# One transformer block on one core: P times V as two row halves among the other half's scores, and 64x32 column tiles for scores, maxima and side products

## The chip, the cores and the metric

The kernel runs on one core of a Trainium2 chip. A time is the device time of one execution in microseconds (us). Before the change two executions took 1753.78 us each. One more execution was profiled; the lines marked as profile come from it. Engines are named as in the profile: PE (TensorE, matmuls), PEld (its weight loads), DVE (VectorE), ACT (ScalarE), POOL (GpSimd) and SP (the queue that starts most DMAs).

## The reference

One block with adaptive layer norm: 2048 tokens of width 512, attention of 32 heads of width 16 that all share one key head and one value head, and a bilinear feed-forward layer of width 1792. Everything is float32.

```python
mod = (silu(c) @ w_mod)                    # six rows: sa, ca, ga, sb, cb, gb
h = layernorm(x) * (1 + ca) + sa
q = (h @ wq) as 32 heads of 16;  k = h @ wk;  v = h @ wv     # one k, one v
p = softmax(q k^T / 4);  x = x + ga * (concat(p v) @ wo)
h = layernorm(x) * (1 + cb) + sb
x = x + gb * (((h @ w_gate) * (h @ w_up)) @ w_down)
```

## The kernel before, in words

The 2048 queries are four blocks of 512. A *unit* is four heads of one block, so there are 32 units, eight for each block. Inside a unit the loop runs over 16 key tiles of 128 keys.

Three kinds of work belong to each unit. First, the **maxima**: for each query row the largest score over all keys, found one unit ahead of its use (`max_mm`, L535). Products of 128 queries by 512 keys go into a bank `mx`, and DVE reduces each bank to one column (L544). Second, the **scores**, transposed, 128 keys by 512 queries for each head (`qk_exp`, L574): a product into a bank `sc` (L579), then ACT's exponential into the tile `P` in SBUF (L581). The maximum is subtracted inside the product, since two of the 50 contracted rows hold it. Third, **P times V** (`pv`, L583): for each key tile, four float32 products, one for each head, each with 32 columns of weights (16 of V, the others of ones for the row sums), accumulate in one bank `pv` (L588). At the end of the unit ACT copies that bank out (`pv_out`, L591), and DMAs carry the parts on.

Queries and keys are held twice in SBUF, on partitions 0 to 63 and 64 to 127, as high and low float16 halves, 48 or 50 rows each. A product of scores or maxima uses the rows of one copy (`a` = 0 or 1) and all 128 columns, so that two of them, one for each half of the rows, can share the array.

The rest, called **side products** here, is dense work: the query projection, the output projection `wo`, and the feed-forward layer. They are float16 in three terms (high by high, low by high, high by low). `duo` (L471) takes two result groups at a time, splits each product's contraction of 128 into two row halves (`half`, L467), and lets one row half work on one group's bank while the other works on the second's; at mid-way the two swap. `plain` (L496) does a product with all 128 rows.

The order is written out by hand: the engines run what the Python code issues, in that order. The main loop at the file's end takes 32 steps in each unit, two for each key tile. In a step it issues a maximum for rows 0, a score for rows 1, a score for rows 0 and a maximum for rows 1. After every second step comes P times V of the key tile before; after the others `fill_gap` (L1039) issues some side products, as many as a credit allows that grows with the work left before a due step (`pace`, L1018). `BURST` caps how many go at once. 38 steps of maxima alone (`LEAD`) run ahead of the main loop, and what is left of the side work, with all of block 3's feed-forward layer, runs behind it.

PSUM has eight banks: two for scores and one `spare` (a third for scores, or the second bank of a `duo`), three for maxima, one `misc`, one for P times V.

Of the kernel before, what the change touches and what calls it, by code (L numbers as in the profile page):

```python
# [31 lines left out]
NMX = 3  # L32
# [7 lines left out]
BURST = 6  # L40
LEAST = 4
# [11 lines left out]
def adaln_mqa_glu_kernel(ctx: ExitStack, tc: tile.TileContext, x_in, wq_in, wk_in, wv_in, wo_in,  # L53
# [20 lines left out]

    def ps_mx():
        return psum.tile([128, 512], F32, name="mx", tag="mx", bufs=NMX)

# [23 lines left out]
    for i in range(6, 8):  # L101
        xts.append(work.tile([128, 2, D], F32, name="P", tag="P", bufs=4))
# [363 lines left out]

    def half(p, g, i, r, start, stop):  # L467
        left, right = g.op(i)
        nc.tensor.matmul(p, left[64 * r:64 * r + 64], right[64 * r:64 * r + 64], start=start, stop=stop)  # L469
# [65 lines left out]
    def max_mm(u, i, a):  # L535
        kc, r = divmod(i, 8)
        p, t = divmod(r, 4)
        s = sst[u % 3]
        if i == 0 and a == 0:
            mparts[u] = work.tile([128, 2, 2, 4, 4], F32, name="mpart")  # L540
        m = ps_mx()
        nc.tensor.matmul(m, s[64 * a:64 * a + 48, p, t * 128:(t + 1) * 128],  # L542
                         kst[64 * a:64 * a + 48, kc * 512:(kc + 1) * 512], start=True, stop=True)
        nc.vector.tensor_reduce(mparts[u][:, a, p, t, kc:kc + 1], m, axis=AX.X, op=OP.max)  # L544
# [29 lines left out]
    def qk_exp(u, kt, p, a):  # L574
        s = sst[u % 3]
        if (u, kt, p) not in ptl:
            ptl[u, kt, p] = work.tile([128, 2, D], F32, name="P", tag="P", bufs=4)
        t = ps_sc()
        nc.tensor.matmul(t, kst[64 * a:64 * a + 50, kt * 128:(kt + 1) * 128],  # L579
                         s[64 * a:64 * a + 50, p, :], start=True, stop=True)  # L580
        nc.scalar.activation(ptl[u, kt, p][:, a, :], t, AF.Exp)  # L581

    def pv(u, kt):  # L583
        if kt == 0:
            pvb[u] = psum.tile([128, 512], F32, name="pv", tag="pv", bufs=1)
        for j in range(4):
            p, a = divmod(j, 2)
            nc.tensor.matmul(pvb[u][32 * j:32 * j + 32, :], vst[:, kt, :], ptl[u, kt, p][:, a, :],  # L588
                             start=(kt == 0), stop=(kt == KT - 1))

    def pv_out(u):  # L591
        b, g = divmod(u, UB)
        ev = work.tile([128, BT], F32, name="ev", tag="ev", bufs=3)
        nc.scalar.activation(ev, pvb[u], AF.Copy, scale=evs)  # L594
# [55 lines left out]
    def wo_work(b):  # L650
# [13 lines left out]
        def fin(t):  # L664
            def f(p):
                if b < NB - 1:
                    x1 = work.tile([128, D], F32, name="x1", tag="x1", bufs=4)
                else:
                    x1 = work.tile([128, D], F32, name="x1p", tag="P", bufs=4)
# [322 lines left out]
    def max_half(a):  # L992
        u, i = divmod(mstep[0], NSTEP)
        if a == 1:
            mstep[0] += 1
# [43 lines left out]
    def fill_gap(step):  # L1039
# [17 lines left out]
        if cur["one"]:  # L1057
            burst(step, max(1, min(int(credit[0]), cur["left"], MOST_ONE)))
            return
        turn = cur["turn"]  # L1060
        parts = max(-(-turn // BURST), min(round(turn / max(credit[0], 1.0)), turn // LEAST), 1)
        n = -(-turn // parts)
        if not cur["second"]:
            n = max(n, -(-cur["turn"] // max((NU * NSTEP - 2 - step) // 2, 1)))
# [64 lines left out]

    for u in range(NU):  # L1130
# [3 lines left out]
        for i in range(NSTEP):  # L1134
# [4 lines left out]
            max_half(0)  # L1139
            qk_exp(u, kt, p, 1)  # L1140
            drain_mids()
            qk_exp(u, kt, p, 0)
            max_half(1)
            if p == 1:
                if kt == 0:
                    if u > 0:
                        pv(u - 1, KT - 1)
                        posts.append(lambda u=u: pv_out(u - 1))
                else:
                    pv(u, kt - 1)  # L1150
                late_max()
            elif fill or cur["gen"]:
                credit[0] = min(credit[0] + pace(step), 9.0)
                one = cur["one"] if cur["gen"] else fill[0][1] == "one"
                if credit[0] >= (MOST_ONE if one else 1.0):
                    fill_gap(step)
            side_step(step)
            if u > 0 and g % 2 == 0 and i in (4, 8, 14):
                if i == 4:
                    nrm = normalise((u - 1) // UB, ((u - 1) % UB) // 2)  # L1160
                nrm[(4, 8, 14).index(i)]()
# [21 lines left out]
    pv(u, KT - 1)  # L1183
# [58 lines left out]
```

## Time and profile before

| what | value |
|---|---|
| the two timed executions | 1753.78 us and 1753.78 us |
| the profiled execution: span from first to last instruction | 1754.7 us |
| instructions in it | 32145, of them 12655 matmuls and 12655 weight loads |
| from the first P times V matmul to the last | 95.9 to 1603.3 us |
| PE busy | 1695.0 us, 97% |
| DVE busy | 1412.2 us, 80% |
| ACT busy | 1220.7 us, 70% |
| POOL busy | 505.0 us, 29% |
| the PE clock granted, mean | 0.988 |

The span is 0.9 us longer than the timed executions, 0.05%, and the view says nothing of time outside it. PE's busy time is the union of the times in which a matmul is under way, with ends that are modelled; 97% says that PE is hardly ever empty, not that it is at its peak. The timeline merges equal instructions that follow one another into one row: its start, its length, the engine, the line, the operation, the tiles, and a count. In a form such as 64\*128 the first number is the rows that a product contracts, the second its weight columns. A float32 product is two matmuls in the trace, so that P times V of one key tile is "x8".

### The profile page before, as it was taken

How to read it: one execution, taken by the hardware profiler on the slowest of the kernel's cores; microseconds unless marked ns; L12 is line 12 of the kernel's file. 1: busy time of each engine (PE TensorE's matmuls, PEld its weight loads, DVE VectorE, ACT ScalarE, POOL GpSimd, SP SyncE). 2: the span in 40 equal slices, each digit the busy share in tenths (PEclk: the TensorE clock that was granted, in tenths of full speed). 3: DMA queues.
4: the chain of work that ended last, by engine and by line, in shares of the span. 5: the costliest groups of instructions: out<-in, count | busy, mean ns of one | idle time of the engine just before them, and what ended most of it. 6: DMA issues, size and time to landing. Idle time of an engine off the chain costs nothing.

```text
span 1754.7 us, 32145 instructions
## 1 busy us (share of the span) xinstructions
PE 1695.0 (97%) x12655; PEld 540.8 (31%) x12655; DVE 1412.2 (80%) x2363; ACT 1220.7 (70%) x2277; POOL 505.0 (29%) x703
## 2 busy tenths in 40 slices
PE   6899899999999999999999999999999999999999
PEld 3222222222223333333223333333223333324444
DVE  7899899999988888888988888888998899920310
ACT  3478788888777777777787777777787777774210
POOL 5714344646576741100031011100031010110330
PEclk9999999999989999999999999999999999999999
DMA  5202121212222200000100000000100000001000
GB/s 197 101 30 85 52 79 55 89 38 91 81 62 60 69 22 9 5 15 19 41 19 16 9 16 9 5 15 18 51 9 16 9 16 9 11 4 41 19 1 24
DMA packets 48899, 66.58 MB, mean 38 GB/s; under 512 B 15270, under 2 KB 29418, under 8 KB 48748
## 3 DMA queue, kind: packets, MB, share of 16 engines
q1 hardware_dynamic: 47164, 64.33, 11.9%
q8 instruction: 99, 1.62, 0.4%
q14 instruction: 52, 0.43, 0.1%
q10 hardware_dynamic: 1584, 0.20, 0.1%
HBM read 51.12 MB, written 8.92 MB: 34 GB/s over the span
## 4 chain that ended last, share of the span: by engine, by line
PE 83%; ACT 7%; DVE 3%; POOL 3%; DMA 2%; issue 1%; SPq 1%; ACTq 0%; POOLq 0%; DVEq 0%
PE pv L588 27%; PE misc L469 18%; PE mx L542 14%; PE sc L579 13%; PE misc L500 9%; ACT P L581 5%; DVE mpart L544 2%; ACT ev L594 1%; POOL h L395 1%; DMA wmA<-in_w_mod_dram 1%; DMA wsl<-in_B_w_gate_dram 0%; ACT qf L510 0%; DVE x L670 0%; PE mxt L556 0%; PE misc L252 0%
## 5 line engine op out<-in xcount | busy, mean ns | idle before, releaser
L544 DVE TENSOR_REDUCE mpart<-mx 128x1 f32<-128x512 f32 x2048 | 1296.1, 682 | 135.8 <-PE sc L579 117.3
L581 ACT ACTIVATE P<-sc 128x512 f32<-128x512 f32 x2048 | 1102.2, 596 | 320.8 <-PE sc L579 311.7
L542 PE MATMUL mx<-kst,sst 48*128 48x512 f16 x2048 | 649.7, 385 | 15.3 <-DVE mpart L544 12.2
L579 PE MATMUL sc<-sst,kst 50*128 50x512 f16 x2048 | 631.7, 383 | 20.9 <-ACT P L581 17.6
L588 PE MATMUL pv<-P,vst 128*32 128x512 f32 x4096 | 552.0, 611 | 0.0
L542 PEld LDWEIGHTS <-sst 48*128 48x128 f16 x2048 | 156.0, 94 | 574.9 <-issue 519.2
L469 PE MATMUL misc<-h2T,wu 64*128 64x512 f16 x1008 | 253.5, 375 | 0.0
L469 PE MATMUL misc<-h2T,wg 64*128 64x512 f16 x1008 | 253.5, 375 | 0.0
L763 POOL TENSOR_SCALAR glu<-gf 128x512 f16<-128x512 f32 x56 | 34.7, 620 | 544.7 <-DVE gf L762 544.7
L579 PEld LDWEIGHTS <-kst 50*128 50x128 f16 x2048 | 138.3, 94 | 80.1 <-issue 40.5
L588 PEld LDWEIGHTS pv<-P,vst 128*32 128x32 f32 x4096 | 81.1, 108 | 173.6 <-issue 168.5
L469 PEld LDWEIGHTS <-wu 64*128 64x128 f16 x1008 | 94.6, 94 | 57.5
L469 PEld LDWEIGHTS <-wg 64*128 64x128 f16 x1008 | 94.3, 94 | 52.4 <-issue 0.9
L762 DVE TENSOR_TENSOR gf<-misc,g 128x512 f32<-128x512 f32 x56 | 38.2, 683 | 86.8 <-PE misc L500 62.9
L469 PE MATMUL misc<-wd,glu 64*128 64x512 f16 x840 | 105.8, 375 | 0.0
L621 POOL TENSOR_TENSOR oc<-oc,rr 128x512 f32<-128x512 f32 x15 | 19.1, 1277 | 257.7 <-DMA sst<-qd 154.2
L756 ACT ACTIVATE g<-misc 128x512 f32<-128x512 f32 x56 | 33.5, 598 | 69.1 <-PE misc L500 63.4
L764 POOL TENSOR_TENSOR glu<-gf,glu 128x512 f16<-128x512 f32 x56 | 64.8, 1157 | 4.7
L469 PEld LDWEIGHTS <-glu 64*128 64x128 f16 x840 | 43.6, 94 | 45.7 <-issue 1.7
L500 PE MATMUL misc<-wd,glu 128*128 128x512 f16 x252 | 55.1, 379 | 0.0
L500 PE MATMUL misc<-h,wq 128*128 128x512 f16 x168 | 51.2, 387 | 0.0
L848 POOL TENSOR_TENSOR kwb<-kwb,wsl 128x448 f32<-128x448 f32 (+1 forms) x40 | 47.5, 1188 | 3.1
(230 smaller groups left out, 886.7 us busy)
## 6 DMA issues: line engine op xcount, KB each, us to landing
wsl<-in_B_w_gate_dram SPq DMA_DIRECT2D x32, 224.0 KB
wsl<-in_B_w_up_dram SPq DMA_DIRECT2D x32, 224.0 KB
wsl<-in_B_w_down_dram SPq DMA_DIRECT2D x28, 256.0 KB
sst<-qd SPq DMA_DIRECT2D x186, 32.0 KB
qd<-q SPq DMA_DIRECT2D x16, 256.0 KB
oc<-ev SPq DMA_DIRECT2D x128, 32.0 KB
rr<-ri SPq DMA_DIRECT2D x16, 256.0 KB
xl<-in_A_x_dram SPq DMA_DIRECT2D x16, 256.0 KB
```

The source lines that it names most:

```text
L469: nc.tensor.matmul(p, left[64 * r:64 * r + 64], right[64 * r:64 * r + 64], start=start, stop=stop)
L500: nc.tensor.matmul(p, left, right, start=i == 0, stop=i == g.n - 1)
L542: nc.tensor.matmul(m, s[64 * a:64 * a + 48, p, t * 128:(t + 1) * 128], kst[64 * a:64 * a + 48, kc * 512:(kc + 1) * 512], start=True, stop= ...
L544: nc.vector.tensor_reduce(mparts[u][:, a, p, t, kc:kc + 1], m, axis=AX.X, op=OP.max)
L579: nc.tensor.matmul(t, kst[64 * a:64 * a + 50, kt * 128:(kt + 1) * 128], s[64 * a:64 * a + 50, p, :], start=True, stop=True)
L581: nc.scalar.activation(ptl[u, kt, p][:, a, :], t, AF.Exp)
L588: nc.tensor.matmul(pvb[u][32 * j:32 * j + 32, :], vst[:, kt, :], ptl[u, kt, p][:, a, :], start=(kt == 0), stop=(kt == KT - 1))
L756: nc.scalar.activation(st["g", f], p, AF.Copy, scale=2.0 ** -45)
L762: nc.vector.tensor_tensor(gf, p, st["g", f], op=OP.mult)
L763: nc.gpsimd.tensor_scalar(st["glu"][:, 0, f, :], gf, 1.0, 0.0, op0=OP.mult, op1=OP.add)
L764: nc.gpsimd.tensor_tensor(st["glu"][:, 1, f, :], gf, st["glu"][:, 0, f, :], op=OP.subtract)
L848: nc.gpsimd.tensor_tensor(acc, acc, t, op=OP.add)
```

## The change

Five things change.

1. P times V is taken in two row halves of 64 keys (`pv(u, kt, r)`). Rows 0 to 63 accumulate in the bank `pv`, rows 64 to 127 in a second bank, `pvb`. At a unit's end ACT copies the first into SBUF (`pv_lower`), and DVE adds the scaled second to it (`pv_out`).
2. A step's two scores and two maxima now all use the same row half, the lower in even steps and the upper in odd ones. Between the two pairs stands P times V of the other row half: of the key tile before in odd steps, of the one before that in even steps.
3. Each product of scores, maxima and `duo` is issued as four, with 32 weight columns each (`quarters`).
4. Banks and buffers: two banks for maxima instead of three (in the lead `pvb` serves as the third), and five `P` tiles instead of four; a tile now holds the two heads that use one copy of the keys.
5. Side products may be issued in every step instead of every second one: `BURST` is 4 instead of 6, `LEAST` 1 instead of 4, the credit grows by half as much for each step, and after a `duo` swaps its banks no side product is issued for two steps. The three steps of normalising move by one.

```diff
-NMX = 3
+NMX = 2
+NP = 5
+CW = 32
...
-BURST = 6
-LEAST = 4
+BURST = 4
+LEAST = 1
...
     def ps_mx():
+        early["n"] += 1
+        if early["on"] and early["n"] % 3 == 0:
+            return psum.tile([128, 512], F32, name="mx", tag="pvb", bufs=1)
         return psum.tile([128, 512], F32, name="mx", tag="mx", bufs=NMX)
...
+    def quarters(p, left, right, start=True, stop=True):
+        for c in range(0, 128, CW):
+            nc.tensor.matmul(p[c:c + CW, :], left[:, c:c + CW], right, start=start, stop=stop)
+
     def half(p, g, i, r, start, stop):
         left, right = g.op(i)
-        nc.tensor.matmul(p, left[64 * r:64 * r + 64], right[64 * r:64 * r + 64], start=start, stop=stop)
+        quarters(p, left[64 * r:64 * r + 64], right[64 * r:64 * r + 64], start, stop)
...
-    def pv(u, kt):
+    def pv(u, kt, r):
         if kt == 0:
-            pvb[u] = psum.tile([128, 512], F32, name="pv", tag="pv", bufs=1)
+            pvb[u, r] = psum.tile([128, 512], F32, name="pv", tag=("pv", "pvb")[r], bufs=1)
+        ks = slice(64 * r, 64 * r + 64)
         for j in range(4):
             p, a = divmod(j, 2)
-            nc.tensor.matmul(pvb[u][32 * j:32 * j + 32, :], vst[:, kt, :], ptl[u, kt, p][:, a, :],
+            nc.tensor.matmul(pvb[u, r][32 * j:32 * j + 32, :], vst[ks, kt, :], ptl[u, kt, a][ks, p, :],
                              start=(kt == 0), stop=(kt == KT - 1))
...
+    def pv_lower(u):
+        evt[u] = work.tile([128, BT], F32, name="ev", tag="ev", bufs=3)
+        nc.scalar.activation(evt[u], pvb[u, 0], AF.Copy, scale=evs)
+
     def pv_out(u):
         b, g = divmod(u, UB)
-        ev = work.tile([128, BT], F32, name="ev", tag="ev", bufs=3)
-        nc.scalar.activation(ev, pvb[u], AF.Copy, scale=evs)
+        ev = evt[u]
+        nc.vector.scalar_tensor_tensor(ev, pvb[u, 1], evs, ev, op0=OP.mult, op1=OP.add)
...
+        if cur["second"] and step < cur["swapped"] + 3:
+            return
...
-            max_half(0)
-            qk_exp(u, kt, p, 1)
+            a = p
+            max_half(a, 0, 2)
+            qk_exp(u, kt, 0, a)
+            if p == 1:
+                if kt:
+                    pv(u, kt - 1, 0)
+                elif u:
+                    pv(u - 1, KT - 1, 0)
+                    posts.append(lambda u=u: pv_lower(u - 1))
+            elif kt > 1:
+                pv(u, kt - 2, 1)
+            elif u:
+                pv(u - 1, KT - 2 + kt, 1)
+                if kt:
+                    posts.append(lambda u=u: pv_out(u - 1))
             drain_mids()
-            qk_exp(u, kt, p, 0)
-            max_half(1)
+            max_half(a, 1, 2)
+            qk_exp(u, kt, 1, a)
```

The order of instructions shows it in two places. The first is PE inside the main loop, with one step that has no side products ahead of P times V and one behind it. `mx` and `sc` are PSUM banks of maxima and scores, `sst1` holds the queries, `kst` the keys, `pv` the sums, `misc` a side group's bank, `glu` and `wd` the operands of the last feed-forward product. Before:

```order
L542 MATMUL mx_16746<-kst_124,sst1_120 128x512
...
L579 MATMUL sc_16750<-sst0_119,kst_124 128x512
...
L579 MATMUL sc_16753<-sst0_119,kst_124 128x512
...
L542 MATMUL mx_16756<-kst_124,sst1_120 128x512
L588 MATMUL pv_16145<-P_16690,vst_117 32x512 x2
L588 MATMUL pv_16145<-P_16711,vst_117 32x512 x2
...
L542 MATMUL mx_16770<-kst_124,sst1_120 128x512
```

With the change, one step of a row half, where each row of L476 stands for four of the same name, for four column tiles:

```order
L476 MATMUL mx_31783<-kst_124,sst2_122 32x512
...
L476 MATMUL sc_31790<-sst1_120,kst_124 32x512
...
L599 MATMUL pv_31397<-P_31641,vst_117 32x512
L599 MATMUL pv_31397<-P_31686,vst_117 32x512
...
L476 MATMUL mx_31800<-kst_124,sst2_122 32x512
...
L476 MATMUL sc_31806<-sst1_120,kst_124 32x512
...
L476 MATMUL misc_31418<-wd_13135,glu_24258 32x512
...
L476 MATMUL misc_31419<-wd_13135,glu_24258 32x512
```

P times V stood alone between two steps, once in a key tile; now half of it stands inside every step, between that step's two pairs of maximum and score, and side products stand behind the second pair.

The second place is DVE at a unit's end. `mpart` takes the maxima, `mm` and `mt` are their last stages, `rc` the reciprocal row sums. Before:

```order
L544 TENSOR_REDUCE mpart<-mx 128x1 x60
L550 TENSOR_REDUCE mm<-mpart 128x16
L544 TENSOR_REDUCE mpart<-mx 128x1 x4
L562 SCALAR_TENSOR_TENSOR mt_3220<-mxt,mt_3219 16x128
L544 TENSOR_REDUCE mpart<-mx 128x1 x26
L612 RECIPROCAL rc<-rc 128x32
```

With the change:

```order
L555 TENSOR_REDUCE mpart<-mx 128x1 x46
L561 TENSOR_REDUCE mm<-mpart 128x16
L555 TENSOR_REDUCE mpart<-mx 128x1 x4
L573 SCALAR_TENSOR_TENSOR mt_5327<-mxt,mt_5326 16x128
L555 TENSOR_REDUCE mpart<-mx 128x1 x14
L611 SCALAR_TENSOR_TENSOR ev<-pv,evs,ev 128x512
L555 TENSOR_REDUCE mpart<-mx 128x1 x14
L629 RECIPROCAL rc<-rc 128x32
```

One addition over a whole bank (L611) stands in DVE's row of maxima once in a unit.

More of the change, by code (lines that the diff above doesn't have):

```diff
@@ L101, in adaln_mqa_glu_kernel @@
     for i in range(6, 8):
-        xts.append(work.tile([128, 2, D], F32, name="P", tag="P", bufs=4))
+        xts.append(work.tile([128, 2, D], F32, name="P", tag="P", bufs=NP))
     for i in range(8):
@@ L541, in max_mm @@
         m = ps_mx()
-        nc.tensor.matmul(m, s[64 * a:64 * a + 48, p, t * 128:(t + 1) * 128],
-                         kst[64 * a:64 * a + 48, kc * 512:(kc + 1) * 512], start=True, stop=True)
+        quarters(m, s[64 * a:64 * a + 48, p, t * 128:(t + 1) * 128],
+                 kst[64 * a:64 * a + 48, kc * 512:(kc + 1) * 512])
         nc.vector.tensor_reduce(mparts[u][:, a, p, t, kc:kc + 1], m, axis=AX.X, op=OP.max)
@@ L575, in qk_exp @@
         s = sst[u % 3]
-        if (u, kt, p) not in ptl:
-            ptl[u, kt, p] = work.tile([128, 2, D], F32, name="P", tag="P", bufs=4)
+        if (u, kt, a) not in ptl:
+            ptl[u, kt, a] = work.tile([128, 2, D], F32, name="P", tag="P", bufs=NP)
         t = ps_sc()
-        nc.tensor.matmul(t, kst[64 * a:64 * a + 50, kt * 128:(kt + 1) * 128],
-                         s[64 * a:64 * a + 50, p, :], start=True, stop=True)
-        nc.scalar.activation(ptl[u, kt, p][:, a, :], t, AF.Exp)
-    def pv(u, kt):
+        quarters(t, kst[64 * a:64 * a + 50, kt * 128:(kt + 1) * 128], s[64 * a:64 * a + 50, p, :])
+        nc.scalar.activation(ptl[u, kt, a][:, p, :], t, AF.Exp)
+    def pv(u, kt, r):
         if kt == 0:
-            pvb[u] = psum.tile([128, 512], F32, name="pv", tag="pv", bufs=1)
+            pvb[u, r] = psum.tile([128, 512], F32, name="pv", tag=("pv", "pvb")[r], bufs=1)
+        ks = slice(64 * r, 64 * r + 64)
         for j in range(4):
             p, a = divmod(j, 2)
-            nc.tensor.matmul(pvb[u][32 * j:32 * j + 32, :], vst[:, kt, :], ptl[u, kt, p][:, a, :],
+            nc.tensor.matmul(pvb[u, r][32 * j:32 * j + 32, :], vst[ks, kt, :], ptl[u, kt, a][ks, p, :],
                              start=(kt == 0), stop=(kt == KT - 1))
+    evt = {}
+    def pv_lower(u):
+        evt[u] = work.tile([128, BT], F32, name="ev", tag="ev", bufs=3)
+        nc.scalar.activation(evt[u], pvb[u, 0], AF.Copy, scale=evs)
     def pv_out(u):
         b, g = divmod(u, UB)
-        ev = work.tile([128, BT], F32, name="ev", tag="ev", bufs=3)
-        nc.scalar.activation(ev, pvb[u], AF.Copy, scale=evs)
+        ev = evt[u]
+        nc.vector.scalar_tensor_tensor(ev, pvb[u, 1], evs, ev, op0=OP.mult, op1=OP.add)
         if g % 2 == 0:
@@ L668, in f @@
                 else:
-                    x1 = work.tile([128, D], F32, name="x1p", tag="P", bufs=4)
+                    x1 = work.tile([128, D], F32, name="x1p", tag="P", bufs=NP)
                 nc.vector.scalar_tensor_tensor(x1, p, sca[:, 7:8], xls[b, t], op0=OP.mult, op1=OP.add)
@@ L990, in drain_mids, with max_half @@
             f()
[L992 to L995, printed above, removed]
+    def max_half(a, j=0, n=1):
+        u, i = divmod(mstep[0] + j, NSTEP)
+        if a == 1 and j == n - 1:
+            mstep[0] += n
         if u >= NU:
@@ L1063, in fill_gap @@
         if not cur["second"]:
-            n = max(n, -(-cur["turn"] // max((NU * NSTEP - 2 - step) // 2, 1)))
+            n = max(n, -(-cur["turn"] // max(NU * NSTEP - 6 - step, 1)))
         burst(step, n)
@@ L1128, in ffn_twos @@
         return gu + twos(down)
+    early["on"] = False
     for u in range(NU):
@@ L1181, in adaln_mqa_glu_kernel @@
     u = NU - 1
-    pv(u, KT - 1)
+    pv(u, KT - 2, 1)
+    pv(u, KT - 1, 0)
+    pv_lower(u)
+    pv(u, KT - 1, 1)
     pv_out(u)
```

19 lines of the change are left out of this document (7 added, 12 removed).

## The prediction

> **What bounds the kernel now.** I read the page's engine shares and chain first, then the windows by stage, then the timeline of single key tiles. The page:
>
> ```profile
> PE 1695.0 (97%) x12655; PEld 540.8 (31%) x12655; DVE 1412.2 (80%) x2363; ACT 1220.7 (70%) x2277; POOL 505.0 (29%) x703
> PE pv L588 27%; PE misc L469 18%; PE mx L542 14%; PE sc L579 13%; PE misc L500 9%; ACT P L581 5%; DVE mpart L544 2%; ACT ev L594 1%; POOL h L395 1%; DMA wmA<-in_w_mod_dram 1%; DMA wsl<-in_B_w_gate_dram 0%; ACT qf L510 0%; DVE x L670 0%; PE mxt L556 0%; PE misc L252 0%
> ```
>
> The chain is PE nearly throughout, with P times V its largest part. The windows (columns: window, its length, busy time and count by engine, clock) tell the stages apart:
>
> ```profile
> 0.00:96.00 96.00, 74.94 (x385) 27.05 (x389) 77.78 (x163) 40.73 (x72) 63.29 (x118) 0.96 0.42 149
> 96.00:443.00 347.00, 332.03 (x2360) 75.33 (x2363) 326.26 (x558) 284.34 (x543) 159.73 (x175) 0.98 0.20 62
> 443.00:1230.00 787.00, 777.09 (x6316) 253.67 (x6312) 690.04 (x1124) 590.55 (x1102) 197.34 (x271) 0.99 0.10 27
> 1230.00:1604.00 374.00, 365.06 (x2897) 118.16 (x2891) 289.82 (x475) 289.92 (x542) 52.00 (x80) 1.00 0.05 15
> 1604.00:1754.70 150.70, 145.90 (x712) 66.58 (x708) 28.35 (x46) 15.19 (x23) 32.63 (x60) 0.99 0.07 24
> ```
>
> From 96 to 443 us (block 0) DVE is busy for 326 of 347 us, so PE is not alone there; from 443 to 1604 it has 181 us of idle time and PE is the bound. The clock is at 0.96 to 1.00, so its granted share explains nothing. A key tile of the PE-bound stage:
>
> ```profile
> 1200.28 0.39 PE L542 MATMUL mx<-kst,sst 48*128 48x512 f16 x1
> 1200.29 0.60 PE L579 MATMUL sc<-sst,kst 50*128 50x512 f16 x2
> 1200.51 0.38 PE L542 MATMUL mx<-kst,sst 48*128 48x512 f16 x1
> 1200.73 1.03 PE L469 MATMUL misc<-wd,glu 64*128 64x512 f16 x8
> 1201.59 0.38 PE L542 MATMUL mx<-kst,sst 48*128 48x512 f16 x1
> 1201.60 0.65 PE L579 MATMUL sc<-sst,kst 50*128 50x512 f16 x2
> 1201.88 0.39 PE L542 MATMUL mx<-kst,sst 48*128 48x512 f16 x1
> 1202.20 1.06 PE L588 MATMUL pv<-P,vst 128*32 128x512 f32 x8
> 1203.20 0.39 PE L542 MATMUL mx<-kst,sst 48*128 48x512 f16 x1
> ```
>
> It lasts 2.92 us. Two products on different row halves start together (1200.28 and 1200.29) and the next two 0.22 later, so a float16 product holds its row half for **0.215** (8 halves, four pairs, from 1200.73 to 1201.59: 0.86). Maxima and scores are eight products, four pairs, 0.86. P times V holds the whole array for 1.00. From the last pair (1201.88, plus 0.215) to 1202.20 there is 0.10 in which nothing streams; the same at its end, as a shorter window shows where its first four start together:
>
> ```profile
> 1202.20 0.64 PE L588 MATMUL pv<-P,vst 128*32 128x512 f32 x4
> 902.28 0.20 PEld L588 LDWEIGHTS pv<-P,vst 128*32 128x32 f32 x8 [0.47 <-issue]
> 12.41 0.23 PEld L274 LDWEIGHTS misc<-wmA,silr 128*32 128x32 f32 x8 [9.50 <-issue]
> ```
>
> Two waves of four in 1.00 less 0.10: a wave is **0.45**. So two changes of tile form cost 0.20 for each key tile, and during P times V no score runs. DVE and ACT set the other floor:
>
> ```profile
> 409.33 7.64 DVE L544 TENSOR_REDUCE mpart<-mx 128x1 f32<-128x512 f32 x12
> 410.77 0.39 PE L542 MATMUL mx<-kst,sst 48*128 48x512 f16 x1
> 413.38 0.39 PE L542 MATMUL mx<-kst,sst 48*128 48x512 f16 x1
> 415.85 0.39 PE L542 MATMUL mx<-kst,sst 48*128 48x512 f16 x1
> 1140.11 1.08 ACT L581 ACTIVATE P<-sc 128x512 f32<-128x512 f32 x2 [0.45 <-PE sc L579]
> ```
>
> With no side product a key tile takes 2.47 (413.38 to 415.85), and DVE reduces without a pause: **1.234 for two maxima**, one step. Two exponentials take 1.08. With two whole products it takes 2.61 (410.77 to 413.38).
>
> **The change, part by part.** Times are for one step, half a key tile.
>
> *Both row halves at once.* A step's four products hold one row half for 4 x 0.215 = 0.86; the half P times V, again eight matmuls, two waves, holds the other for 0.90. Roles alternate, so each row half has 1.76 of work in two steps: **0.88**, and 0.90 if the two must end together. I take 0.89. Before, the same work took (0.86 + 0.90 + 0.20)/2 = 0.98. The form changes vanish, except around whole products (0.19 in such a step). The trace does not show a float32 matmul streaming beside float16 ones. Bounds: 0.88 if they don't disturb each other; 1.10 if the order stands in the way (first rival).
>
> *Side products.* Four column tiles of a half side by side should last what the half lasted: V's projection, 32 columns wide, shows it.
>
> ```profile
> 87.42 0.83 PE L442 MATMUL pv<-h,wv 128*32 128x512 f16 x12
> 88.19 0.44 PE L542 MATMUL mx<-kst,sst 48*128 48x512 f16 x2
> ```
>
> Twelve matmuls in 0.77 to the next form: three rounds of 0.215 and one change of form. So 0.215 for each side product, as now. The loads are four times as many and lie behind the matmuls, eight of them within 0.20 to 0.23 in the rows above; if a step's 24 were not hidden, it would be the third rival.
>
> *The pattern of steps.* A step lasts the longer of 0.89 + 0.215 n, with n side products, and 1.234. Counted in the order of the changed kernel, the 1021 intervals between halves of P times V hold:
>
> - n = 0: 345 with maxima at 1.234, 25 at the end without at 1.08: 453
> - two whole products: 84 at 0.89 + 0.43 + 0.19 = 1.51: 127
> - n = 1: 34 at 1.23: 42
> - n = 2: 287 at 1.32: 379
> - n = 3: 104 at 1.535: 160
> - n = 4: 142 at 1.75: 249
>
> Sum **1410**. The same for the kernel before: five and six side products to a key tile take
>
> ```profile
> 1136.60 0.39 PE L542 MATMUL mx<-kst,sst 48*128 48x512 f16 x1
> 1139.65 0.39 PE L542 MATMUL mx<-kst,sst 48*128 48x512 f16 x1
> 1126.92 0.39 PE L542 MATMUL mx<-kst,sst 48*128 48x512 f16 x1
> 1130.18 0.39 PE L542 MATMUL mx<-kst,sst 48*128 48x512 f16 x1
> L588 PE MATMUL pv<-P,vst x4096: 592/617/1062, 95.9 to 1603.3; 128*32 128x512 f32 x196
> ```
>
> 3.05 and 3.26, and its order holds 91 key tiles without any, 84 with two whole ones, 211 with four, 46 with five, 78 with six: 225 + 219 + 616 + 140 + 254 = 1454. Its loop, from the first P times V to the last, was 1507. So 53 lie in what the classes leave out: transposes, layer norms, starts of blocks. I carry them over, since the change touches none. Bounds: 0 to 53, taken at 53.
>
> *Buffers between steps.* DVE can finish a lagging reduction while PE goes on by at most two banks of maxima. The order often holds two empty steps between n = 2 and n = 4; in such a pair I let DVE catch up by 0.15, some 75 times: -11. Bounds: 0 and, with perfect smoothing, -68 (second rival).
>
> *Fewer banks.* A third bank for maxima is gone. With two, a maximum may start when the last but one is reduced. In a step of 1.32 the two maxima start 0.43 and 0.89 apart; a reduction needs 0.62. The first of them is reduced about 1.05 after its start (0.43 from matmul to reduction, 1200.28 to the row below, then 0.62), ahead of the next step's first. No stall above n = 0, and there DVE is the bound anyway. A blocked maximum would hold all PE work behind it; I put it at 0.
>
> ```profile
> 1200.71 2.59 DVE L544 TENSOR_REDUCE mpart<-mx 128x1 f32<-128x512 f32 x4 [0.32 <-PE sc L579]
> L670 DVE SCALAR_TENSOR_TENSOR x<-misc,sca,xl 128x512 f32<-128x512 f32 x12 | 8.9, 741 | 0.8 <-PE misc L469 0.5 <-issue 0.3
> ```
>
> *A second bank of sums.* DVE adds 32 operations of the form of L670's, 0.74 each. In the PE-bound units they hide in DVE's idle time; in block 0's eight units they cost 8 x 0.74 = **+6** (24 if nothing hid them anywhere). The order leaves more than a step between the addition and the bank's next use. ACT's copy stays; the DMAs of a unit are as many as before and start a step later or earlier.
>
> *The tail.* The order issues 1488 side products inside the loop where it had 1566, so 78 more run behind it. There a product of 128 rows takes 0.216:
>
> ```profile
> 1610.36 8.38 PE L500 MATMUL misc<-wd,glu 128*128 128x512 f16 x38
> ```
>
> Thirty-eight in 8.38, the last one's drain included. 78 x 0.216 = **+17**. The start is DVE's work and stays.
>
> **The sum.** Loop: 1410 + 53 - 11 - 1507 = -55. With the tail and block 0: -55 + 17 + 6 = **-32** on a span of 1754.7. The timed runs are 0.9 below that span: 1753.8 - 32, about **1722 us**. The gain is small because DVE's 1.234 takes it away in 345 steps, and because the side products keep their price.
>
> **Rivals.**
>
> *Order kept strictly: slower.* PE would start matmuls only in the order issued. Then a step's first maximum starts at 0, its score at 0.215 with P times V's first wave beside it, and the second wave at 0.67. Only then may the second maximum start, and its score at 0.88. That pair ends at 1.10, the waves at 1.12. A step is 1.10 + 0.215 n, and the classes sum to 453 + 144 + 45 + 439 + 182 + 279 = 1542: loop 1542 + 42 - 1507 = +77, in all +100: **1854 us**. It decides as soon as a step has one side product. Against it speaks P times V itself: its four products are eight matmuls, the two halves of one product next to each other in the built program, yet the first four starts fall together. A matmul does pass one that waits for its tile. What is not shown is passing eight. [...]
>
> *DVE and PE smooth each other: much faster.* If no empty step costs more than PE's 0.89, blocks 1 to 3 lose another 57: **1665 us**. For it: DVE's 181 us of idle time. Against it: two banks are too few to store a step.
>
> *Issue becomes the bound: slower.* A step has 24 pairs of load and matmul in 0.89, 37 ns for a pair. Against it: eight loads, each with its matmul, are through within 0.23, at most 29 ns for a pair, and that right after an idle time of 9.50 us, when nothing could have been issued ahead. The longest dense stretch, twelve pairs in 0.77, is 64 ns each, explained by streaming. At 40 ns a step is 0.96, each side product 0.32, and the loop grows by 1488 x 0.105 + some 40: **about 1920 us**. It decides from 37 ns on. [...]
>
> **How the numbers follow.** Overlap as worked out: 0.63, own range 1695 to 1755. Smoothing: 0.17. Strict order: 0.14. Issue: 0.06. The range is 1655 to 1830: it takes in smoothing and leaves out most of the two slow cases. A difference of 2% (35 us) is about what a measurement of this kernel can tell from none: below 1719 lie smoothing and 0.26 of the first case, 0.43; within 2% lie 0.36 of it; above 1789 the slow cases and 0.01, 0.21.
>
> **What would show it.** In steps without side products DVE should reduce without a pause, 2.47 for four. In steps with two, matmuls of `mx` and `sc` should start while L599's are under way, and a step should take 1.32. The changes of form, 0.10 each, should be gone. PE's second pair of a step tells the first rival: it should start 0.43 after the first, not 0.67. The forecast is wrong if steps of n = 2 take over 1.45, if DVE pauses in empty steps, or if the tail grows by more than 17.

## The result, and the profile after

The changed kernel takes 1829.47 us (two executions, 1829.22 and 1829.71) where the kernel before takes 1753.78: 1.043 times as long, with a 95% interval of 1.040 to 1.0461. The forecast was 1722 us and faster. The time lies at the upper edge of its range; the direction was wrong, by 107 us.

The page of the changed kernel, engine shares and the chain that ended last by engine and by line:

```profile
PE 1741.3 (95%) x38027; PEld 851.7 (47%) x38027; DVE 1468.0 (80%) x2395; ACT 1283.0 (70%) x2277; POOL 504.5 (28%) x703
...
PE 75%; DVE 14%; POOL 3%; issue 3%; DMA 2%; ACT 2%; SPq 0%; DVEq 0%; ACTq 0%; POOLq 0%
PE pv L599 22%; PE misc L476 17%; PE mx L476 15%; DVE mpart L555 11%; PE misc L511 10%; PE sc L476 9%; DVE gf L779 1%; ACT P L591 1%; DVE ev L611 1%; DMA wsl<-in_B_w_gate_dram 1%; DMA wmA<-in_w_mod_dram 1%; PE misc L730 0%; POOL wsl L958 0%; PE misc L259 0%; DVE bs L695 0%
```

P times V has lost part of its share (27% before), and DVE has gained: 14% where it had 3%, and 11 of the 14 are the reductions of the maxima (L555). PE now waits for DVE in the chain. The windows by stage (the same columns as before):

```profile
97.00:443.00 346.00, 324.57 (x5766) 109.87 (x5759) 309.07 (x506) 271.88 (x483) 134.63 (x142) 0.99 0.19 56
443.00:1230.00 787.00, 762.44 (x20044) 419.70 (x20043) 698.92 (x1116) 609.07 (x1081) 223.91 (x306) 1.00 0.12 32
1230.00:1660.00 430.00, 415.96 (x10680) 219.02 (x10657) 354.46 (x569) 344.78 (x619) 51.93 (x80) 1.00 0.07 17
```

In the stage where DVE was nearly full, it is now busy for 309 of 346 us, not 326 of 347. Less DVE work is done in the same time, so the program is behind. The first score of each unit tells where. From the start of one unit's first score to the next unit's, added up by block (the last unit has no successor):

| block | before | after |
|---|---|---|
| 0 | 347 us | 384 us |
| 1 | 393 us | 403 us |
| 2 | 393 us | 404 us |
| 3, seven units | 331 us | 339 us |

Half of the loss is in block 0, whose only side products are whole ones. From the last P times V to the end it is 164 us, 12 more than before (forecast 17 more).

What the change was built for does happen. One step of the last stage, with the products of `mx` and `sc` on one row half and P times V (L599) on the other:

```profile
1246.72 0.40 PE L476 MATMUL mx<-kst,sst 48*32 48x512 f16 x4
1246.90 0.61 PE L599 MATMUL pv<-P,vst 64*32 64x512 f32 x4
1246.94 0.40 PE L476 MATMUL sc<-sst,kst 50*32 50x512 f16 x4
1247.16 0.40 PE L476 MATMUL mx<-kst,sst 48*32 48x512 f16 x4
1247.33 0.61 PE L599 MATMUL pv<-P,vst 64*32 64x512 f32 x4
1247.38 0.40 PE L476 MATMUL sc<-sst,kst 50*32 50x512 f16 x4
```

All eight matmuls of P times V are issued ahead of the second maximum, yet that starts at 1247.16 and the second wave at 1247.33: in these rows a matmul passes earlier ones, whose tiles the first wave (from 1246.90) still holds. The second score starts 0.44 behind the first, as forecast (0.43).

Now a step is measured from its first score to the next step's first score, and sorted by what the order of the changed kernel puts into it:

| steps | count | forecast | mean measured | excess in all |
|---|---|---|---|---|
| n = 0, with maxima | 345 | 1.234 | 1.386 | 53 us |
| two whole products | 84 | 1.51 | 1.76 | 21 us |
| n = 1 | 34 | 1.23 | 1.31 | 3 us |
| n = 2 | 287 | 1.32 | 1.464 (median 1.39) | 41 us |
| n = 3 | 104 | 1.535 | 1.82 (median 1.70) | 29 us |
| n = 4 | 142 | 1.75 | 1.81 (median 1.79) | 8 us |

Some 40 of these 155 us stand in the 61 steps that also hold transposes or sums over weights, 0.5 to 0.7 each; that is the part which the forecast carried over from before as 53. Most of the excess of n = 2 and n = 3 lies in 52 steps alone, those in which a pair of side groups begins. The timeline of all engines at such a step:

```profile
655.94 0.60 ACT L773 ACTIVATE g<-misc 128x512 f32<-128x512 f32 x1 [0.16 <-PE misc L476]
656.00 0.69 DVE L555 TENSOR_REDUCE mpart<-mx 128x1 f32<-128x512 f32 x1 [0.29 <-PE misc L476]
...
656.59 0.40 PE L476 MATMUL misc<-h2T,wg 64*32 64x512 f16 x4
656.64 0.69 DVE L779 TENSOR_TENSOR gf<-misc,g 128x512 f32<-128x512 f32 x1
657.24 0.68 DVE L555 TENSOR_REDUCE mpart<-mx 128x1 f32<-128x512 f32 x1
657.38 0.40 PE L476 MATMUL misc<-h2T,wu 64*32 64x512 f16 x4 [0.40 <-DVE gf L779]
...
657.81 0.40 PE L476 MATMUL mx<-kst,sst 48*32 48x512 f16 x4
```

The new pair's second bank (657.38) is the one that DVE's product of gate and up (L779) still reads, and that stood behind a reduction. The next maximum, issued behind the pair's first product, starts at 657.81, though it has nothing to do with that bank, and its own was free once the reduction of 656.00 had ended (656.69). Block 0 shows another wait, in all rows of DVE and some of PE for one key tile:

```profile
267.69 2.63 DVE L555 TENSOR_REDUCE mpart<-mx 128x1 f32<-128x512 f32 x4 [0.39 <-PE mx L476]
268.43 0.40 PE L476 MATMUL mx<-kst,sst 48*32 48x512 f16 x4
...
269.18 0.40 PE L476 MATMUL mx<-kst,sst 48*32 48x512 f16 x4
...
269.72 0.60 PE L511 MATMUL misc<-h,wq 128*128 128x512 f16 x2
...
270.26 0.40 PE L476 MATMUL mx<-kst,sst 48*32 48x512 f16 x4
...
270.71 2.63 DVE L555 TENSOR_REDUCE mpart<-mx 128x1 f32<-128x512 f32 x4 [0.39 <-PE mx L476]
```

DVE reduces four banks without a pause and then has no full bank left: the maximum of 270.26 had to wait until the whole products (269.72) were through, and only two banks had been filled ahead. The key tile takes 3.02 us, where 2.74 were forecast (1.51 and 1.234); 3.02 is also the median of the 84 key tiles with whole products, and in 77 of them DVE pauses for more than 0.1 in the empty step.

### The profile page after: what moved, and what is told of

Same layout as the page of the kernel before. It is cut to its first block, busy times and chain, and to the rows that moved or that the text cites. A ratio compares the mean times of both kernels' runs of the same rounds, so it can differ in the third digit from the quotient of the medians.

```text
span 1827.4 us, 83987 instructions
## 1 busy us (share of the span) xinstructions
PE 1741.3 (95%) x38027; PEld 851.7 (47%) x38027; DVE 1468.0 (80%) x2395; ACT 1283.0 (70%) x2277; POOL 504.5 (28%) x703
## 4 chain that ended last, share of the span: by engine, by line
PE 75%; DVE 14%; POOL 3%; issue 3%; DMA 2%; ACT 2%; SPq 0%; DVEq 0%; ACTq 0%; POOLq 0%
PE pv L599 22%; PE misc L476 17%; PE mx L476 15%; DVE mpart L555 11%; PE misc L511 10%; PE sc L476 9%; DVE gf L779 1%; ACT P L591 1%; DVE ev L611 1%; DMA wsl<-in_B_w_gate_dram 1%; DMA wmA<-in_w_mod_dram 1%; PE misc L730 0%; POOL wsl L958 0%; PE misc L259 0%; DVE bs L695 0%
## 5 line engine op out<-in xcount | busy, mean ns | idle before, releaser
L555 DVE TENSOR_REDUCE mpart<-mx 128x1 f32<-128x512 f32 x2048 | 1330.2, 686 | 155.3 <-PE mx L476 85.3
L599 PE MATMUL pv<-P,vst 64*32 64x512 f32 x8192 | 1081.5, 599 | 0.0
L476 PE MATMUL mx<-kst,sst 48*32 48x512 f16 x8192 | 809.1, 383 | 38.9 <-DVE mpart L555 26.3
L476 PE MATMUL sc<-sst,kst 50*32 50x512 f16 x8192 | 816.4, 379 | 3.3 <-ACT P L591 2.3
L476 PEld LDWEIGHTS <-sst 48*32 48x32 f16 x8192 | 310.8, 91 | 546.0 <-issue 467.0
L476 PE MATMUL misc<-h2T,wu 64*32 64x512 f16 x4032 | 287.5, 376 | 14.5 <-DVE gf L779 14.4
L476 PE MATMUL misc<-h2T,wg 64*32 64x512 f16 x4032 | 293.7, 376 | 0.0
L476 PEld LDWEIGHTS <-kst 50*32 50x32 f16 x8192 | 249.5, 92 | 74.4 <-issue 30.4
L599 PEld LDWEIGHTS pv<-P,vst 64*32 64x32 f32 x8192 | 197.6, 105 | 15.3 <-ACT P L591 0.8
L476 PEld LDWEIGHTS <-wu 64*32 64x32 f16 x4032 | 114.6, 92 | 58.2 <-issue 26.2
L476 PEld LDWEIGHTS <-wg 64*32 64x32 f16 x4032 | 113.9, 92 | 39.6 <-issue 11.3
L476 PE MATMUL misc<-wd,glu 64*32 64x512 f16 x2688 | 116.2, 376 | 3.1 <-DVE x L794 1.7
L779 DVE TENSOR_TENSOR gf<-misc,g 128x512 f32<-128x512 f32 x56 | 38.6, 690 | 85.2 <-PE misc L511 62.9
L476 PEld LDWEIGHTS <-glu 64*32 64x32 f16 x2688 | 60.9, 92 | 28.8 <-issue 5.7
```

The source lines that it names most:

```text
L476: nc.tensor.matmul(p[c:c + CW, :], left[:, c:c + CW], right, start=start, stop=stop)
L599: nc.tensor.matmul(pvb[u, r][32 * j:32 * j + 32, :], vst[ks, kt, :], ptl[u, kt, a][ks, p, :], start=(kt == 0), stop=(kt == KT - 1))
L779: nc.vector.tensor_tensor(gf, p, st["g", f], op=OP.mult)
```

## The experiments

Ratios are to the kernel before, which takes 1754 to 1759 us on the chips used; the changed kernel's is 1.043. Differences in us are differences of ratios times 1754; below some 5 us they can't be told from none.

### Where a pair starts, whole products, and two banks in the kernel before

The first theory was the wait of 657.38, the second that a change of form costs more now, since the overlapped P times V runs dry first; the rival of both was the missing bank of maxima.

```diff
-        if not fill or (fill[0][1] == "one" and step < cur["wait"]):
+        if not fill or step < cur["wait"]:
```

> The changed kernel, but a pair of side groups starts at the earliest three steps after the last one ended (before: in the very next step). First theory, a pair starts before its two banks have been read out, PE waits for them, and everything behind waits too: the 52 first steps lose their excess of about 0.9 us, -48; the later start packs the side products more tightly (empty steps 345 to 439, steps with four 142 to 257), at the measured medians +14. In all -34: about 1795 us. Rival, the loss is that of two banks of maxima instead of three and is spread over all steps: no gain, only the tighter packing, about 1843 us.

Ratio 1.0494 (1.0473 to 1.0516), 1842.6 us: no gain, the number of the rival. The wait at the start is gone, as the waits of the two kernels show (us in all, how often, the longest). The changed kernel:

```profile
PE mx L476 <- DVE mpart L555: 26.3, 72, 1.2
...
PE misc L476 <- DVE gf L779: 15.7, 38, 0.7
```

With the later start the second of these rows no longer appears, and the first has grown:

```profile
PE mx L476 <- DVE mpart L555: 36.9, 94, 1.3
```

By classes, the excess of n = 2 and n = 3 falls by 53 us (steps with transposes left aside), but the empty steps, 439 now, have a mean of 1.437 and not 1.386, and having more empty steps and more steps of four, in place of steps of two, costs more by itself. The wait moved, and the edit gave nothing.

```diff
-        fill.extend(([0, 0], "one", one, QDUE) for one in two)
+        fill.append(([0, 0], "duo", two, QDUE))
```

> The changed kernel, but the query projections of the main loop, 168 products of 128 rows in 84 steps, are issued as pairs of groups in row halves and column tiles like the other side products, so that these steps change no tile form. Second theory, a change of form waits until the overlapped P times V has run dry: the 84 steps go from 1.81 to about 1.39 us, -35, and seven more pairs start, +6: about 1800 us. Rival, those steps are long because DVE or the evacuations of block 0 bound them: at most -5, about 1825 us.

Ratio 1.0371 (1.0349 to 1.0393), 1821.1 us, 10 less than the changed kernel: near the rival. All 84 whole-product steps are gone, with their changes of form, yet block 0 goes only from 384 to 379 us. The form of its side products is not what mainly holds block 0: even with both edits, in the next kernel, it takes 371 us.

> Both edits of the two kernels beside it. If the two causes are separate the gains add up: -34 and -35, about 1760 us. If one covers the other, the larger of the two alone: about 1795 us.

Ratio 1.042 (1.0398 to 1.0442), 1829.9 us: not 1760, and the changed kernel's time. The first two theories fall as causes of the whole.

```diff
-NMX = 3
+NMX = 2
```

> The kernel before with two banks of maxima instead of three, the third left unused, nothing else changed. By the forecast's term for fewer banks nothing changes: 1754 us, give or take 4. Rival, two banks are what holds the changed kernel back: at least +40, about 1795 us or more.

Ratio 1.0775 (1.0748 to 1.0802), 1892.2 us, 136 more than before: one unused bank costs more than the whole change. Key tiles, from P times V to P times V, medians of the two traces:

| key tile | three banks | two banks |
|---|---|---|
| no side products | 2.47 | 3.07 |
| two whole products | 2.61 | 3.07 |
| four side products | 2.91 | 3.07 |
| five | 3.05 | 3.07 |
| six | 3.27 | 3.27 |

Two banks put a floor of 3.07 under each key tile of that order. The timeline of one, PE and DVE:

```profile
434.14 0.38 PE L542 MATMUL mx<-kst,sst 48*128 48x512 f16 x1
434.33 2.48 DVE L544 TENSOR_REDUCE mpart<-mx 128x1 f32<-128x512 f32 x4
...
435.07 0.37 PE L542 MATMUL mx<-kst,sst 48*128 48x512 f16 x1
...
435.67 0.37 PE L542 MATMUL mx<-kst,sst 48*128 48x512 f16 x1
435.97 1.07 PE L588 MATMUL pv<-P,vst 128*32 128x512 f32 x8
...
436.97 0.39 PE L542 MATMUL mx<-kst,sst 48*128 48x512 f16 x1
```

The third maximum (435.07) waits until the first of the four reductions has ended (434.33 plus 0.62), the fourth (435.67) for the second; P times V behind it waits too, and while it runs DVE empties both banks. So the missing bank can be dear; whether it is in the changed order, the next two kernels tell.

### The third bank in the changed kernel

Three banks of maxima beside both halves of P times V would make nine banks; the changed kernel uses eight, by its own layout, and no kernel here uses more. These two kernels leave out two heads, so that the halves share a bank at the same length of a wave; they differ in the use of the freed bank alone.

```diff
-        for j in range(4):
+        for j in range(2):
...
-            nc.tensor.matmul(pvb[u, r][32 * j:32 * j + 32, :], vst[ks, kt, :], ptl[u, kt, a][ks, p, :],
+            c = 64 * r + 32 * j
+            nc.tensor.matmul(pvb[u][c:c + 32, :], vst[ks, kt, :], ptl[u, kt, a][ks, p, :],
...
-NMX = 2
+NMX = 3
```

(The last two lines are the second kernel's.)

> Control for the next kernel. P times V is taken for two of the four heads only, the lower key half into partitions 0 to 63 and the upper into 64 to 127 of one bank, so that one of the two banks of sums is left unused; the exponent is scaled by a quarter, so that half sums stay finite. A wave still holds its row half for 0.45 us, DVE's addition falls away (-10), and the one bank has to be emptied within a step at each unit's end (up to +30): 1820 to 1850 us.

> The kernel beside it (two heads of P times V left out, exponent scaled by a quarter), with the freed bank as a third one for maxima. Third theory, with two banks PE and DVE wait for each other at every step in which the one or the other is late (a side group's evacuation on DVE, a burst of side products on PE), and cannot make it up: 60 to 100 us less than the control, about 1755 us. Rival, the forecast's term: two banks are enough, within 8 us of the control.

The control has a ratio of 1.0464 (1.0446 to 1.0482), the kernel with three banks 1.0048 (1.0031 to 1.0064): **73 us less** for the bank, within the 60 to 100 of the third theory. Blocks 0 to 2 go from 385, 406 and 407 us to 335, 400 and 398, and the seven units of block 3 from 342 to 333: 50 of it in block 0, 6 to 9 us in each other block. The window of block 0, first the control:

```profile
97.00:443.00 346.00, 321.78 (x4846) 106.26 (x4835) 304.20 (x498) 269.36 (x481) 133.81 (x142) 0.99 0.19 55
```

With three banks:

```profile
97.00:443.00 346.00, 335.08 (x5617) 129.92 (x5608) 332.17 (x577) 293.83 (x561) 164.64 (x181) 1.00 0.22 66
```

DVE is busy for 332 of 346 us, with 28 more. In the timeline of two key tiles the whole products come around after 2.42 us, and DVE reduces nine banks without a pause (the 0.90 ahead of them lie at a unit's start, where PE waits 0.39, until 263.75, for ACT to empty the one bank of sums):

```profile
264.88 5.53 DVE L555 TENSOR_REDUCE mpart<-mx 128x1 f32<-128x512 f32 x9 [0.90 <-PE mx L476]
...
265.60 0.61 PE L511 MATMUL misc<-h,wq 128*128 128x512 f16 x2
...
268.02 0.60 PE L511 MATMUL misc<-h,wq 128*128 128x512 f16 x2
```

The whole-product steps still take 1.76, but the empty ones between them 0.96 on the mean of block 0's 143 without transposes, where the control has 1.25: a maximum lies ready while PE is at the whole products, and DVE does not stop for them. The median key tile with whole products takes 2.42.

```diff
-        nc.vector.tensor_reduce(mparts[u][:, a, p, t, kc:kc + 1], m, axis=AX.X, op=OP.max)
+        nc.vector.tensor_reduce(mparts[u][:, a, p, t, kc:kc + 1], m[:, 0:256], axis=AX.X, op=OP.max)
...
-        nc.scalar.activation(ptl[u, kt, a][:, p, :], t, AF.Exp)
+        nc.scalar.activation(ptl[u, kt, a][:, p, :], t, AF.Exp, scale=0.25)
```

> The changed kernel, DVE reducing only 256 of the 512 columns of each bank of maxima (some 0.35 us instead of 0.65), the exponent scaled by a quarter so that nothing overflows; PE's work is unchanged. Third theory, the steps of none and of two side products are held by DVE and its two banks: at 0.89 plus 0.2155 for each side product, with the whole-product steps and the transposes as measured, the loop falls by about 185: 1645 us. Rival, PE itself (loads, changes of form, waits for banks of side groups) holds the steps: 1800 us or more.

Ratio 0.9918 (0.9897 to 0.994), 1742.7 us, 90 less than the changed kernel: DVE matters, but by half of what was expected. The empty steps without transposes fell from 1.32 to 1.10, not to 0.89. In a run of them ACT now has no pause:

```profile
434.39 3.67 ACT L591 ACTIVATE P<-sc 128x512 f32<-128x512 f32 x7
```

Seven exponentials in 3.67 us, 1.05 for the two of a step: with DVE out of the way ACT is the bound, which the expectation had left out. Most of the excess of n = 2 and n = 3, where the pairs start, stayed, too (26 and 21 us, against 37 and 26 in the changed kernel, steps with transposes left aside).

### Adding the edits up, and a bank for block 0 alone

> Three banks of maxima (with two heads of P times V left out and the exponent scaled by a quarter, as in the two kernels with one bank of sums), and both earlier edits: a pair of side groups starts three steps after the last one, and the main loop's query projections are pairs in row halves. If the three causes make up the whole difference from the forecast, the 45 us of the first steps and 25 of the 37 us of the whole-product steps now go as well, less 14 for tighter packing and 10 for DVE's evacuations: 1765 - 46, about 1720 us. Rival, these waits only move to the steps behind, as they did with two banks: 1755 us or more.

Ratio 1.0093 (1.0074 to 1.0112), 1772.0 us: 8 more than with three banks alone. The rival holds; both edits only move waits here too. With three banks the whole products are no more of a burden than pairs: block 0 takes 335 us with them and 351 with both edits.

```diff
+        early["third"] = "spare" if b == 0 else None
...
-            spare["scores"] = not spare["held"] and (cur["gen"] is None or cur["one"]) and not (fill and fill[0][1] == "duo" and open_gate(step))
+            spare["scores"] = b > 0 and not spare["held"] and (cur["gen"] is None or cur["one"]) and not (fill and fill[0][1] == "duo" and open_gate(step))
```

> The changed kernel, whole and exact, but in block 0, where no pair of side groups is under way, the bank called spare serves as the third bank of maxima instead of as the third for scores. Third theory, and the unit times of the two kernels with one bank of sums: block 0 goes from 384 to about 337 us, the others stay: 1783 us. Rival, the third bank helps in all blocks alike, or it was the bank of scores that block 0 needed: 1815 us or more.

Ratio 1.0299 (1.028 to 1.0317), 1808.3 us: 23 us less, between both expectations. Block 0 goes from 384 to 365 us and the other blocks stay. What is missing against 335 may be the price of the bank taken away from the scores; that is argued from these two numbers and was not tried by itself.

The next kernel keeps this block 0 and takes all else from before. Its diff is long; its core:

```diff
+            if b == 0:
...
+                max_half(a, 0, 2)
+                qk_exp(u, kt, 0, a)
...
+            else:
+                max_half(0)
+                qk_exp(u, kt, p, 1)
...
+                    pv_whole(u, kt - 1)
```

> Both kernels in one: block 0 as in the change, with the bank called spare as the third bank of maxima; the lead and blocks 1 to 3 as before the change, with the second bank of sums as the third of maxima there, and the schedule of side products of before. If block 0 takes 335 instead of 347 us and the others what they took before: 1742 us, 0.993 of before. Rival, block 0 gains nothing once DVE sets it, and the hand-over between the two orders costs 2 to 5 us: 1754 to 1760 us.

Ratio 1.0119 (1.0104 to 1.0135), 1777.4 us: slower than before by 21. Its blocks take 363, 396, 393 and 333 us (seven units), against 347, 393, 393 and 331 before: blocks 1 to 3 are those of before, and block 0 is that of the kernel with `spare`, not the 335 that the expectation had put in. No kernel with the whole computation came out below the one before.

### The rest in blocks 1 to 3

With three banks 1765 us were reached; the forecast is 43 below. One suspect was DVE's other work in the row of the maxima.

```diff
-                nc.vector.tensor_tensor(gf, p, st["g", f], op=OP.mult)
+                nc.scalar.activation(gf, p, AF.Copy)
+                nc.gpsimd.tensor_tensor(gf, gf, st["g", f], op=OP.mult)
...
-        nc.vector.scalar_tensor_tensor(ev, pvb[u, 1], evs, ev, op0=OP.mult, op1=OP.add)
+        ev2 = work.tile([128, BT], F32, name="ev2", tag="ev2", bufs=1)
+        nc.scalar.activation(ev2, pvb[u, 1], AF.Copy, scale=evs)
+        nc.gpsimd.tensor_tensor(ev, ev, ev2, op=OP.add)
```

> The changed kernel, whole and exact, with DVE's work beside the maxima moved away: the product of gate and up (56 of 0.69 us) and the addition of the second bank of sums (32 of 0.74 us) are each an ACT copy out of PSUM and a POOL operation instead. Fourth theory, what blocks 1 to 3 lose beyond the forecast are DVE's evacuations, which stand in one row with the maxima: 42 and 31 of them lie in the loop, 52 us; 30 to 50 us less, about 1790 us. Rival, ACT's row (two exponentials of 0.54 us in a step) takes their place, or the wait is the age of the bank and not DVE's work: 1820 to 1840 us.

> The same, and a pair of side groups starts three steps after the last one, as in the first kernel of the study (1842.6 us). Fourth theory: there the wait had moved from the first steps to the empty ones (their excess rose from 25 to 57 us), because DVE still had to do the evacuation; without it the excess falls back and 30 to 50 us go: about 1800 us. Rival, ACT or the packing holds it: 1835 us or more.

Ratios 1.046 (1.044 to 1.048) and 1.0455 (1.0437 to 1.0474), 1836.6 and 1835.7 us: the fourth theory falls. The wait for the bank has only another name, as the waits of the first show:

```profile
PE misc L476 <- ACT gf L781: 22.6, 38, 1.2
```

It is as frequent as DVE's was (38 times) and longer (22.6 us in all against 15.7). ACT has no more room in a step than DVE: two exponentials and a copy of 0.60 are over 1.6. So the last kernels shorten the evacuation itself on both engines.

```diff
-                nc.scalar.activation(st["g", f], p, AF.Copy, scale=2.0 ** -45)
+                nc.scalar.activation(st["g", f][:, 0:64], p[:, 0:64], AF.Copy, scale=2.0 ** -45)
...
-                nc.vector.tensor_tensor(gf, p, st["g", f], op=OP.mult)
+                nc.vector.tensor_tensor(gf[:, 0:64], p[:, 0:64], st["g", f][:, 0:64], op=OP.mult)
```

> The changed kernel, but ACT's copy of gate and DVE's product of gate and up read 64 of the 512 columns of their banks (POOL repeats the 64; the other columns of the result are left out): some 0.2 us each instead of 0.60 and 0.69. Fifth theory, what blocks 1 to 3 lose are these evacuations on both engines: ACT has two exponentials (1.08) and DVE two reductions (1.234) in a step, so an evacuation fits in no empty step, and the next pair waits for it. First steps lose 0.5 of their 0.9, 42 times, the empty steps some 5: 25 us less, about 1805 us. Rival, the bank's age and the order of the step decide, not how long the evacuation takes: 1822 us or more.

> The same part left out, and a pair starts three steps after the last one (1842.6 us with whole evacuations). Fifth theory: the empty steps, whose excess had risen to 57 us, fall back by 25 to 35: about 1812 us. Rival, the tighter packing alone holds it: 1835 us or more.

> The same part left out, with one bank of sums and three of maxima (two heads of P times V left out, exponent scaled by a quarter; 1764.8 us with whole evacuations). Fifth theory: 25 to 30 us less, about 1737 us, near the forecast. Rival: 1758 us or more.

Ratios 1.0309 (1.0287 to 1.0332), 1.0399 (1.038 to 1.0418) and 0.994 (0.9918 to 0.9962): 21, 17 and 19 us less than with whole evacuations, 1808.6, 1825.4 and 1744.0 us. The fifth theory had 25, 25 to 35 and 25 to 30. The waits for `gf` are all but gone in the first:

```profile
PE misc L476 <- DVE gf L779: 0.4, 2, 0.2
```

So the length of the evacuations of gate and up costs 17 to 21 us, wherever the pair starts.

### Tiles of another form

```diff
-CW = 32
+CW = 64
```

> The changed kernel with 64 columns in each tile of scores, maxima and side products; P times V keeps 32. Second theory, a tile of another form waits until all of the old form has run dry, so nothing of P times V overlaps: a step is 0.86 + 0.90 + 0.20 with half of the array idle, some 2600 us. Rival, only the 0.10 of each of two changes is paid for and the overlap stays: about 2030 us. Third possibility, forms run beside one another freely: 1830 us or a little less, with half as many loads.

> The changed kernel with whole products of 64x128 for scores, maxima and side products, as before the change; P times V keeps 64x32. If a wave of P times V runs only when no tile of another form is in the array, a step without side products has two pairs of products (0.43), two changes of form (0.20) and two waves (0.90), some 1.55 us at the full clock, as in the kernel with 64 columns, and the time is far above 2000 us again. Rival, it was the 64 columns, and 128 run beside P times V: below 1900 us. If the granted clock again falls in block 0, where DVE leaves PE without a pause, that was no accident of one run.

2915.7 and 2879.3 us, one execution each. In the timeline of the second, PE's rows in the stage from 1650 to 2240 us, with a granted clock of 0.94:

```profile
1796.09 1.06 PE L599 MATMUL pv<-P,vst 64*32 64x512 f32 x8
1797.08 0.39 PE L476 MATMUL mx<-kst,sst 48*128 48x512 f16 x1
...
1798.18 0.38 PE L476 MATMUL sc<-sst,kst 50*128 50x512 f16 x1
1798.49 1.06 PE L599 MATMUL pv<-P,vst 64*32 64x512 f32 x8
1799.49 0.39 PE L476 MATMUL mx<-kst,sst 48*128 48x512 f16 x1
```

From 1796.09 to 1797.08 and from 1798.49 to 1799.49 no matmul starts but those of P times V, one row half alone, for 0.99 and 1.00; the score ahead of it starts 0.31 earlier, 0.215 and 0.10 for the change of form. With equal forms (the rows of 1246.72) they overlap. So these rows agree with the second theory's premise, that a tile of another form waits until the old form has run dry. The times themselves say less, since the clock was at 0.50 from 130 to 1050 us (last section).

## Why the prediction was wrong

**What failed: "Fewer banks. ... I put it at 0".** The step asked whether a single stall arises in a step of 1.32, and found none. But the third bank's work is another: it lets DVE fall behind in one step and catch up in the next. In block 0 a whole-product step, in which PE is late, is followed by an empty one, in which DVE is. With two banks such a key tile takes 3.02 us (forecast 2.74); with three it takes 2.42 in the rows shown. The bank is worth 73 of the 107 us, 50 of them in block 0. Of the empty steps the prediction said "there DVE is the bound anyway"; in block 0 with two banks DVE ran out of full banks and was busy for 309 of 346 us.

**The same fault in the classes.** Each class was given the longer of PE's and DVE's time, so by that pricing a further bank could only have made the kernel faster than forecast (the second rival). That DVE's 1.234 holds only while PE brings its maxima in time was not asked. In blocks 1 to 3 the forecast let DVE catch up by 11 us with two banks; nothing of the kind is seen, since no class lies below its forecast, and so the second rival did not come either.

**What was not seen: the start of a pair.** The schedule of side products lets a pair begin in the step right after the last, when its banks are still being read. The 52 steps in which that happens carry most of the excess of n = 2 and n = 3. Yet undoing it gave nothing, as far as the sums tell because ACT and DVE have no step in which 0.6 to 0.7 us of evacuation fit: ACT's 1.08 and DVE's 1.234 already fill an empty step. The length of the evacuations is worth 17 to 21 us. "I carry them over, since the change touches none" covered these starts without a look.

**What was right.** The overlap itself and PE's passing of waiting matmuls (second pair after 0.44, forecast 0.43), so strict order is refuted; a wave of P times V held its row half for 0.43 (1246.90 to 1247.33, forecast 0.45); n = 4 at a median of 1.79 (forecast 1.75), n = 2 at 1.39 (1.32; the limit was 1.45), each side product 0.20; 38,027 pairs of load and matmul are no bound, as n = 4 shows (by the third rival's numbers it would take 0.96 plus 4 x 0.32, or 2.24), so issue is refuted. The tail grew by 12, not over 17. Change of form: 0.31 less 0.215 is the 0.10 that was used. DVE's additions, +6, can't be told apart: the control without them is no faster.

**What the test said.** A pause of DVE in empty steps was named as a sign of being wrong; in block 0 DVE pauses for 0.1 to 0.39 in the empty step behind the whole products in 77 of 84 cases. A step of n = 2 over 1.45 was another; the mean is 1.464, the median 1.39.

**The account.** Of 107 us, 73 are the bank and 17 to 21 the evacuations. The kernel with three banks and short evacuations takes 1744 us, 22 above the forecast; those 22 stay open (some 6 of them may be the control's own distance to the changed kernel, 1.0464 against 1.043, which lies within the intervals). The value of the bank was measured with two heads of P times V left out. With all four heads a third bank was tried in block 0 alone, taken from the scores, for 23 us; for all blocks it was not tried, since the changed kernel's layout already uses eight banks.

## What to carry to other kernels

Count PSUM banks by how far one engine may run ahead of the other, not by whether a stall appears in the average step: where steps alternate between two bounds, a missing bank can take away the catching up between them, here 73 us, and 136 in the order before. A class of steps priced at the longest of its engines' times assumes that the others are never late for it. When a wait can be moved but not removed, look at whether the engine behind it has a step with room for the work.

## What the hardware showed that was not expected

In the rows shown P times V, in tiles of 64 rows and 32 columns, runs among maxima and scores of 48 and 50 rows where these have 32 columns too: its first wave starts at 1246.90, between the maximum of 1246.72 and the score of 1246.94. With 128 columns beside its 32 no other matmul starts for 0.99 (from 1796.09), and with 64 as well: there P times V runs alone from 1796.03 to 1797.02, 0.99.

And the granted clock was 0.50 where PE was hardly ever empty. Windows of the kernel with 128 columns:

```profile
130.00:600.00 470.00, 469.83 (x1694) 58.16 (x1696) 176.78 (x277) 153.08 (x271) 72.23 (x75) 0.50 0.08 24
...
1650.00:2240.00 590.00, 587.69 (x4329) 140.45 (x4323) 384.02 (x589) 319.95 (x567) 51.87 (x80) 0.94 0.04 12
```

From 130 to 1050 us the clock is 0.50, and PE is busy for 469.83 of 470 us in the first part of it (to 600) and for 449.78 of 450 in the second; the kernel with 64 columns shows the same 0.50 there. The fall itself is not theirs alone: the changed kernel, too, is at 0.50 from 97 to 103 us, but at 1.00 from 104 to 130. Over the first 130 us it has a mean of 0.93, the kernels with 128 and 64 columns 0.83 and 0.84. In its block 0 it has 0.99, with PE busy for 324.57 of 346. What in these two kernels keeps the clock low was not settled.
